# Fourier mixing followed by an ELU layer, one core: exponentials moved ahead of fold copies and conversions in ScalarE's order of the first sixteen steps

## Chip, cores and metric

The kernel runs on one core of one Trainium2 chip. The metric is the device time of one execution in microseconds (us). The kernel before took 1987.27 us in the median of three runs (1987.22 to 1990.91). The profiled execution, a run of its own, took 1994.49 us and its profile spans 1992.7 us.

## The reference

```python
X = np.fft.fft(x, axis=1)            # x: 8 x 3008 x 256
X = np.fft.fft(X, axis=2).real       # rows of 256, 24064 of them
h = X.reshape(B * S, D) @ w_in       # 256 -> 2048
g = np.where(h > 0.0, h, np.exp(np.minimum(h, 0.0)) - 1.0)
return (g @ w_out).astype(np.float32)    # 2048 -> 256
```

The two weight matrices arrive as 64-bit floats and are turned into 32-bit floats by the kernel itself.

## The kernel before, in words

**Stages.** For each batch of 3008 rows, the rows are folded by symmetry (additions and subtractions of loaded rows), and a Fourier transform along the sequence is made as matrix products with cosine and sine tables. Its results go into ring buffers in SBUF (Rr and Ir, with Rb for one channel more). The transform along the 256 channels is folded into the first weight matrix: products of channel tables with w_in give Wc and Ws ("fold chunk", L367), which ScalarE copies out of PSUM (put_chunk, L381) and of which one row is sent through DRAM to become the column vector wex (spread_last_row, L386: a transfer wx, then a transfer wex that waits for it).

**Steps.** The main loop has 376 steps. A step takes 256 columns of a ring and two of the sixteen blocks of 128 hidden units: matmuls P and Q (L693, L698) make the even and odd parts H in PSUM, VectorE makes E (L710) between them and the difference (h_minus, L720) after them, ScalarE makes two Relu (below_plus, below_minus) and two exponentials (exp_plus, exp_minus), and VectorE makes two ELU results (g_plus, g_minus, L736). Two steps after its start the results are multiplied by w_out into the PSUM accumulators pA to pD. Steps from 16 on use a scheme with seven products and four sums on GpSimd (L767 to L781); steps 0 to 15 are "side by side": two column tiles take turns, and each multiplies plainly (mm_plain, L803), pA and pB for one tile, pC and pD for the other. Tiles share buffers: PSUM bank M is single, H has three banks.

**Conversions.** In steps 0 to 14 the 64-bit weights are converted, one chunk of 256 hidden units in most steps (class Chunk, L173): `fields` (two VectorE operations, L211 and L217), `power` (three ScalarE operations), `round` (GpSimd, L359), `scale` (VectorE L254, then GpSimd L359). Chunk c of w_out is needed by the plain matmuls that stand in step 2c+2.

**Order.** Every call is an event with a due time in units of a step T = 4.8 (`at`, L1010); the events are sorted by due time (L1270) and the compute instructions of each engine run in that order. The due times are only a sorting key. Waits between engines are semaphores set by the program's dependences. DMA issues are not pinned, so that a scheduler places them: on SyncE's queue (SP) and, for the indirect loads of x and for the first chunk's wx and wex, on GpSimd's.

**Other work in the first 28 steps.** The odd transform of batch 0 (R_odd) goes through pA and pB ahead of their use by the main loop. Batch 1 is loaded (load_x, L137) and folded on GpSimd in 38 pieces spread over steps (begin_folds, L1192; loop from L1237 on). A separate path makes the transform of one channel for all batches (the "extra rows"): GpSimd adds two rows rx (L1212), SyncE spreads them and then gathers single channels of x with sixteen slow transfers (load_ext, L554), writes them to DRAM and reads them back as xs; GpSimd makes xe from xs (fold_ext, L587, due in step 25), and TensorE transforms xe (dft_ext, L612, at the end of step 25).

Of the kernel before, what the change touches and what calls it, by code (L numbers as in the profile page):

```python
# [77 lines left out]
def kernel(  # L78
# [58 lines left out]
    def load_x(b):  # L137
        L = [
            spool.tile([128, 6 * ND], FP, tag=f"xl{j}", bufs=1, name=f"xl{j}")
            for j in range(4)  # L140
        ]
        for j in (2, 1):
            c = 1 if j == 2 else 2 if b == NB - 1 else 0
            nc.gpsimd.indirect_dma_start(
                out=L[j],
                out_offset=None,
                in_=xflat,
                in_offset=bass.IndirectOffsetOnAxis(
                    ap=ix[:, c : c + 1].bitcast(U32), axis=0
                ),  # L150
                element_offset=b * SEQ * ND,
            )
        nc.sync.dma_start(out=L[3], in_=xrows(b, HALF, 6, 128))
        nc.sync.dma_start(out=L[0], in_=xrows(b, 0, 6, 128))
        if b == NB - 1:
            nc.gpsimd.dma_start(
                out=L[1][0:1, 0 : 5 * ND], in_=xrows(b, SEQ - 5, 1, 1, 5)
            )
        return L
# [184 lines left out]
    def bank(tag):  # L344
        bufs = 3 if tag == "H" else 1
        return ppool.tile([128, 512], FP, tag=tag, bufs=bufs, name=tag)
# [20 lines left out]
    def fold_chunk(c):  # L367

        q, half = divmod(c, 2)
        ps = folds[c] = bank("H")  # L370
        for n, part in enumerate((128, 0)):
            for h in range(2):
                mm(
                    ps[:, 256 * n : 256 * n + 256],
                    CC[:, h * 256 + part : h * 256 + part + 128],
                    w1[q][:, h, half * 256 : half * 256 + 256],
                    n == 0 and h == 0,
                    h == 1,
                )

    def put_chunk(c):  # L381
        cols = slice(c * 256, (c + 1) * 256)
        for n, dst in enumerate((Ws, Wc)):
            act(dst[:, cols], folds[c][:, 256 * n : 256 * n + 256])

    def spread_last_row(q):  # L386
        c = slice(q * 256, (q + 1) * 256)
        queue = nc.sync if q else nc.gpsimd
        queue.dma_start(out=wx_dr[:, c], in_=Ws[127:128, c])
        with nc.allow_non_contiguous_dma(reason="one row to columns"):  # L390
            queue.dma_start(
                out=wex[:, 2 * q : 2 * q + 2],
                in_=wx_dr[:, c].rearrange("o (f p) -> p (o f)", p=128),
            )
# [263 lines left out]
    def spread_ext(b, kodd):  # L658
        for sl, a, z in ring_cut(b * HALF + kodd * RUN, RUN, False):
            a, z = a + kodd * RUN, z + kodd * RUN  # L660
            nc.sync.dma_start(
                out=Rb[:, sl],
                in_=r128_dr[b : b + 1, a:z].to_broadcast([128, z - a]),
            )
            nc.sync.dma_start(out=Ir[127:128, sl], in_=r128_dr[b : b + 1, a:z])
# [137 lines left out]
    def mm_plain(i, a):  # L803

        S = steps[i]
        q = i // 8
        if i % 8 == 0 and a == 0:
            tiles[q] = Tile()
            tiles[q].acc = [bank(t) for t in ACC[2 * q : 2 * q + 2]]
        for n, (half, sign) in enumerate(((0, a), (1, 1 - a))):  # L810
            for r in range(2):
                mm(
                    tiles[q].acc[a][:, n * TW : (n + 1) * TW],
                    w2b(i, r, half),
                    blk(S, 2 * sign + r),
                    i % 8 == 0 and n == 0 and r == 0,
                    i % 8 == 7,
                )
        if a:
            del steps[i]  # L820
# [181 lines left out]
    def dft_now(d, par, tag):  # L1002
        d.mms(par, bank(tag))

    R_even, I_even = Dft(0, 0, 0, EO[0]), Dft(1, 0, 0, EO[2])
    R_odd, I_odd = Dft(0, 0, 1, EO[1]), Dft(1, 0, 1, EO[3])
# [3 lines left out]
    def at(t, fn):  # L1010
        events.append((t, len(events), fn))
# [58 lines left out]
    T = PERIOD  # L1070
    for chunk, k in (
        (w2_chunks[0], 0),
        (w1_chunks[2], 1),
        (w1_chunks[3], 2),
        (w2_chunks[1], 3),
        (w1_chunks[4], 4),
        (w2_chunks[2], 5),
        (w1_chunks[5], 6),
        (w2_chunks[3], 7),
        (w1_chunks[6], 8),  # L1080
        (w2_chunks[4], 9),
        (w1_chunks[7], 10),
        (w2_chunks[5], 11),
        (w2_chunks[6], 12),
        (w2_chunks[7], 14),
    ):
        t = k * T + 1.0
        at(t, chunk.fields)
        at(t + 0.02, chunk.power)
        at(t + 0.05, chunk.round)  # L1090
        at(k * T + (3.7 if k else 1.9), chunk.scale)
    for chunk, t in (
        (w1_chunks[6], 0.95),
        (w1_chunks[7], 2.2),
# [6 lines left out]
    for c in range(1, 8):  # L1101
        t = max(2 * c - 3, c % 3) * T + 4.7 if c > 1 else 2.3
        at(t, lambda c=c: fold_chunk(c))
        t = max(2 * c - 2, 3) * T + 1.4 if c > 1 else 3.0
        at(t, lambda c=c: put_chunk(c))
        at(t + 0.01, lambda c=c: spread_last_row(c))
    for i in range(8):
# [11 lines left out]
    for slot in range(total):  # L1119
        i = slot % 2 * 8 + slot // 2 if slot < 16 else slot  # L1120
        t = slot * T
        for dt, fn in (
            (0.0, mm_P),
            (0.9, even_part),
            (2.17, mm_Q),
            (3.55, h_minus),
            (4.2, below_plus),
            (4.8, below_minus),
            (T + 1.5, exp_plus),
            (T + 2.2, g_plus),  # L1130
            (T + 2.21, exp_minus),
            (T + 2.9, g_minus),
        ) + (
            (
                (2 * T + 0.87, lambda i: mm_plain(i, 0)),
                (2 * T + 3.04, lambda i: mm_plain(i, 1)),
            )
            if i < 16
            else WINOGRAD
        ):  # L1140
            at(t + dt, lambda fn=fn, i=i: fn(i))
# [12 lines left out]
    for q in range(2, n_tiles):  # L1154
        t = (8 * q + 9) * T
# [6 lines left out]
    def safe(col):  # L1162

        return 8 * ((col - 1 - RING) // TW) + 8 if col > RING else 0
# [16 lines left out]
    def at_dft(step, gap, b, ri, kodd, stat):  # L1181
        box = []

        def d():
            if not box:
                box.append(Dft(ri, b, kodd, stat()))
            return box[0]

        at_half(step, d, 1, 0)
        at_half(step + gap, d, 0, b * HALF + (kodd + 1) * RUN)  # L1190

    def begin_folds(b):  # L1192
        state["EO"], state["ops"] = fold_x(state["L"], lambda key: nc.gpsimd, 2)

    steps_b = HALF * 8 // TW
    for t, fn in (
        (-1.8, I_even.copy),
        (0.0, I_even.plus),
        (0.1, I_even.minus),
        (3.1, lambda: dft_now(R_odd, 1, "pA")),  # L1200
        (3.2, lambda: dft_now(R_odd, 0, "pB")),
        (T + 0.95, R_odd.copy),
        (T + 1.0, R_odd.plus),
        (T + 1.1, R_odd.minus),
    ):
        at(t, fn)
    at_half(4, lambda: I_odd, 1, 0)
# [6 lines left out]
    for n in range(16):  # L1214
        j, k = divmod(n, 4)
# [13 lines left out]
    n_big = sum(k[0] not in "czx" for k, _ in fold_keys)  # L1229
    for b in range(1, NB):  # L1230
        s0 = (b - 1) * steps_b
        l0 = s0 - 8 if b > 1 else 7.2
        at(l0 * T + 0.1, lambda b=b: state.update(L=load_x(b)))
        f0, f1 = (s0 - 1, s0 + 38) if b > 1 else (11, 37)
        at(f0 * T, lambda b=b: begin_folds(b))
        n = 0
        for key in fold_keys:  # L1237
            at(
                int(f0 + n * (f1 - f0) / n_big) * T + 1.3,
                lambda key=key: state["ops"][key](),  # L1240
            )
            n += key[0][0] not in "czx"
        for n, (ri, kodd) in enumerate(((0, 0), (1, 0), (0, 1), (1, 1))):
            at_dft(
                s0 + (28, 34, 38, 42)[n], 2, b, ri, kodd,
                lambda k=2 * ri + kodd: state["EO"][k],
            )
        for kodd in range(2):
            step = s0 + (28, 38)[kodd]
            assert step >= safe(b * HALF + (kodd + 1) * RUN)  # L1250
            at(step * T + 1.0, lambda b=b, kodd=kodd: spread_ext(b, kodd))
# [50 lines left out]
```

## Time and profile before

| quantity | us |
|---|---|
| span of the profiled execution | 1992.7 |
| TensorE matmuls busy | 1963.4 |
| VectorE busy | 1263.0 |
| ScalarE busy | 870.0 |
| GpSimd busy | 1330.9 |
| TensorE busy between 50 and 150 | 92.73 of 100 |
| TensorE busy between 150 and 186 | 36.00 of 36 |
| TensorE busy between 186 and 222 | 30.13 of 36 |
| TensorE busy between 400 and 800 | 400.00 of 400 |

A line of the timeline gives the start, the duration, the engine, the line of the kernel, the operation, the tile written and the tiles read, the count that was merged, and in square brackets how long the engine had been idle and what ended that. PE is TensorE, DVE VectorE, ACT ScalarE, POOL GpSimd, SPq the DMA issues of SyncE. A matmul of 32-bit floats shows as two records, and records overlap because the pipeline does: the pace is read from start to start. A line of the waits reads: who waited, for what, microseconds in total, times, the longest.

### The profile page before, as it was taken

The numbers are of one execution on the slowest core, as the hardware profiler recorded it, in microseconds if no ns is written. First come the engines' busy times: TensorE is split into PE (matmuls) and PEld (weight loads), VectorE is DVE, ScalarE is ACT, GpSimd is POOL, SyncE is SP. The second block draws the span as 40 slices with busy tenths as digits, with TensorE's granted clock in tenths as the row PEclk, the third lists the DMA queues.
The fourth block names the chain that finished last, engine by engine and source line by source line (L and its number), as shares of the span: only waits on it lengthen the run. The fifth ranks groups of instructions, "written<-read, shape, count | busy, mean of one in ns | idle before, by whom it ended". The sixth has DMA issues, their size and how long they took to land.

```text
span 1992.7 us, 26822 instructions
## 1 busy us (share of the span) xinstructions
PE 1963.4 (99%) x8896; PEld 1664.4 (84%) x8896; DVE 1263.0 (63%) x2322; ACT 870.0 (44%) x1666; POOL 1330.9 (67%) x1804
## 2 busy tenths in 40 slices
PE   8999999999999999999999999999999999999998
PEld 5777888888888888888888888888888888888887
DVE  6565656666566665666666765666556665566665
ACT  3553434444344434444434443444434444344443
POOL 3377757777487765777567775677757776455655
PEclk9999999999999999999999999999999999999999
DMA  9147401120101211011101211002010110100101
GB/s 352 33 20 13 106 11 17 27 75 16 16 15 37 59 23 18 16 46 44 26 14 19 59 29 28 12 19 83 11 21 12 19 22 14 16 12 12 22 10 23
DMA packets 255740, 71.08 MB, mean 36 GB/s; under 512 B 244255, under 2 KB 245044, under 8 KB 255090
## 3 DMA queue, kind: packets, MB, share of 16 engines
q1 hardware_dynamic: 251026, 56.53, 15.1%
q0 software_dynamic: 2400, 12.59, 1.9%
q8 instruction: 70, 1.15, 0.2%
q14 instruction: 68, 0.56, 0.1%
q10 hardware_dynamic: 2176, 0.26, 0.1%
HBM read 44.50 MB, written 24.80 MB: 35 GB/s over the span
## 4 chain that ended last, share of the span: by engine, by line
PE 90%; DMA 3%; DVE 2%; SPq 2%; ACT 1%; issue 1%; POOL 1%; POOLq 0%; DVEq 0%; ACTq 0%
PE H L350 36%; PE pB L350 15%; PE pD L350 15%; PE pC L350 15%; PE pA L350 8%; SPq L560 1%; DMA x<-in_x_dram 1%; DMA xl<-in_x_dram,ix 1%; DVE E L710 1%; SPq L920 0%; DMA wx<-Ws 0%; SPq L577 0%; DVE G L720 0%; POOL w L359 0%; ACT pow L362 0%
## 5 line engine op out<-in xcount | busy, mean ns | idle before, releaser
L359 POOL TENSOR_TENSOR G<-G 128x256 f32<-128x256 f32 x1440 | 1036.5, 729 | 565.4 <-DVE G L736 454.8
L710 DVE SCALAR_TENSOR_TENSOR E<-Rb,wex,H 128x256 f32<-128x256 f32 x752 | 327.8, 477 | 617.0 <-PE H L350 612.4
L362 ACT ACTIVATE G<-H 128x512 f32<-128x512 f32 x376 | 224.6, 597 | 946.1 <-DVE G L720 946.1
L350 PE MATMUL H<-Ir,Ws 128*128 128x256 f32 x1504 | 387.6, 380 | 3.7 <-DVE E L710 3.7
L350 PE MATMUL H<-Rr,Wc 128*128 128x256 f32 x1504 | 387.0, 380 | 0.0
L350 PE MATMUL pC<-G,WT 128*128 128x256 f32 x1440 | 369.5, 379 | 0.0
L350 PEld LDWEIGHTS H<-Rr,Wc 128*128 128x128 f32 x1504 | 285.6, 190 | 54.6 <-issue 3.1
L350 PEld LDWEIGHTS H<-Ir,Ws 128*128 128x128 f32 x1504 | 278.0, 189 | 53.2 <-DVE E L710 6.2
L350 PEld LDWEIGHTS pC<-G,WT 128*128 128x128 f32 x1440 | 273.6, 190 | 37.2
L736 DVE SCALAR_TENSOR_TENSOR G<-G,H 128x512 f32<-128x512 f32 x376 | 255.8, 680 | 53.8 <-ACT G L362 53.8
L720 DVE SCALAR_TENSOR_TENSOR G<-E,H 128x512 f32<-128x512 f32 x376 | 257.1, 684 | 37.7 <-POOL G L359 2.5
L736 DVE SCALAR_TENSOR_TENSOR G<-M,G 128x512 f32<-128x512 f32 x376 | 256.8, 683 | 0.0
L350 PE MATMUL pA<-G,w 128*128 128x256 f32 x784 | 230.9, 381 | 8.6 <-POOL w L359 6.5
L362 ACT ACTIVATE G<-G 128x512 f32<-128x512 f32 x376 | 233.3, 620 | 0.0
L350 PE MATMUL pD<-G,w 128*128 128x256 f32 x784 | 229.3, 379 | 0.0
L350 PE MATMUL pB<-G,w 128*128 128x256 f32 x784 | 229.3, 379 | 0.0
L362 ACT ACTIVATE M<-G 128x512 f32<-128x512 f32 x376 | 223.9, 596 | 0.0
L362 ACT ACTIVATE M<-M 128x512 f32<-128x512 f32 x376 | 220.9, 587 | 0.1
L350 PE MATMUL pB<-G,WT 128*128 128x256 f32 x720 | 214.5, 380 | 1.6 <-POOL G L359 1.6
L350 PE MATMUL pD<-G,WT 128*128 128x256 f32 x720 | 214.4, 379 | 1.5 <-DVE v L356 1.5
L350 PEld LDWEIGHTS pA<-G,w 128*128 128x128 f32 x784 | 149.0, 191 | 31.1 <-POOL w L359 10.9
L350 PEld LDWEIGHTS pD<-G,w 128*128 128x128 f32 x784 | 149.0, 190 | 20.3
(127 smaller groups left out, 1370.7 us busy)
## 6 DMA issues: line engine op xcount, KB each, us to landing
out_dram<-ot SPq DMA_DIRECT2D x496, 32.0 KB
xl<-in_x_dram SPq DMA_DIRECT2D x16, 768.0 KB
MC<-dft_mats SPq DMA_DIRECT2D x4, 1131.0 KB
out_dram<-ot SPq DMA_DIRECT2D x256, 2.0 KB
Rb<-r SPq DMA_DIRECT2D x10, 376.0 KB
raw<-in_moe_w_in_dram SPq DMA_DIRECT2D x7, 512.0 KB
raw<-in_moe_w_out_dram SPq DMA_DIRECT2D x5, 512.0 KB
out_dram<-ot SPq DMA_DIRECT2D x64, 28.0 KB
```

Source lines behind the costliest of these rows:

```text
L350: nc.tensor.matmul(out_, lhsT=lhsT, rhs=rhs, start=start, stop=stop, skip_group_check=True)
L359: pin(nc.gpsimd.tensor_tensor(out=o, in0=a, in1=b, op=op))
L362: pin(nc.scalar.activation(out=o, in_=i, func=func, **kw))
L560: nc.sync.dma_start(out=t[:, s0:s1], in_=bass.AP(tensor=xt, offset=x.offset + row * ND + 128, ap=[[SEQ * ND, NB], [step * ND, s1 - s0], [1 ...
L710: nc.vector.scalar_tensor_tensor(out=S.E[:, c], in0=Rb[:, cols(i)], scalar=wex[:, f : f + 1], in1=S.H[:, c], op0=ALU.mult, op1=ALU.add,)
L720: nc.vector.scalar_tensor_tensor(out=two(S.G[:, 0:512])[:, :, ::-1], in0=two(S.E), scalar=2.0, in1=two(S.H), op0=ALU.mult, op1=ALU.subtract,)
L736: nc.vector.scalar_tensor_tensor(out=o, in0=e, scalar=-1.0, in1=h, op0=ALU.add, op1=ALU.max)
```

## The change

Six edits, all in due times. (1) `fields`, `power`, `round` and `scale` of a conversion in step k move from 1.0, 1.02, 1.05 and 3.7 of that step to -0.5, 0.05, 0.06 and 2.95. (2) put_chunk and spread_last_row of chunks 2 to 7 move from 1.4 to 0.03 of their step. (3) For steps 0 to 15, exp_plus moves from T+1.5 to T+0.01 and exp_minus from T+2.21 to T+0.02. (4) The two halves of the odd transform move from 3.1 and 3.2 to T+0.5 and T+2.5, its copy from T+0.95 to T+2.6, its sum and difference from T+1.0 to T+4.2. (5) Batch 1's load moves from step 7.2 to 5.2. (6) Its folds are spread from step 8 on instead of step 11 on, to step 37 in both.

```diff
-        t = k * T + 1.0
-        at(t, chunk.fields)
-        at(t + 0.02, chunk.power)
-        at(t + 0.05, chunk.round)
-        at(k * T + (3.7 if k else 1.9), chunk.scale)
+        t = k * T
+        at(t - 0.5 if k else 0.95, chunk.fields)
+        at(t + 0.05 if k else 0.96, chunk.power)
+        at(t + 0.06 if k else 0.97, chunk.round)
+        at(t + 2.95 if k else 1.9, chunk.scale)
...
-        t = max(2 * c - 2, 3) * T + 1.4 if c > 1 else 3.0
+        t = max(2 * c - 2, 3) * T + 0.03 if c > 1 else 3.0
         at(t, lambda c=c: put_chunk(c))
         at(t + 0.01, lambda c=c: spread_last_row(c))
...
-            (T + 1.5, exp_plus),
+            (T + 0.01 if slot < 16 else T + 1.5, exp_plus),
             (T + 2.2, g_plus),
-            (T + 2.21, exp_minus),
+            (T + 0.02 if slot < 16 else T + 2.21, exp_minus),
...
-        (3.1, lambda: dft_now(R_odd, 1, "pA")),
-        (3.2, lambda: dft_now(R_odd, 0, "pB")),
-        (T + 0.95, R_odd.copy),
-        (T + 1.0, R_odd.plus),
-        (T + 1.1, R_odd.minus),
+        (T + 0.5, lambda: dft_now(R_odd, 1, "pA")),
+        (T + 2.5, lambda: dft_now(R_odd, 0, "pB")),
+        (T + 2.6, R_odd.copy),
+        (T + 4.2, R_odd.plus),
+        (T + 4.21, R_odd.minus),
...
-        l0 = s0 - 8 if b > 1 else 7.2
+        l0 = s0 - 8 if b > 1 else 5.2
...
-        f0, f1 = (s0 - 1, s0 + 38) if b > 1 else (11, 37)
+        f0, f1 = (s0 - 1, s0 + 38) if b > 1 else (8, 37)
```

In the order that results, each engine runs the same compute instructions as before. On ScalarE a side-by-side step now reads: two exponentials of the step before, fold copies, the conversion's three operations, then the two Relu of its own step. On VectorE the conversion's L254 comes ahead of h_minus instead of behind it, and `fields` ahead of E instead of behind it. On TensorE the odd transform's first half stands between P and Q of step 1 and its second half between Q of step 1 and P of step 2; both stood ahead of P of step 1. On SyncE the raw load of w_in's chunk 7 now comes ahead of the wex transfer of chunk 1, and batch 1's two row loads come behind it. On GpSimd one indirect load of batch 2 (L144) now stands between the xs and the xe operations of the extra rows, and the second one a step ahead of the two rx operations of step 28 instead of behind them.

## The prediction on record

> **What bounds the kernel now.** I read the page first, then TensorE's waits, then the timeline where those waits lie. On the page TensorE is busy for nearly all of the span:
>
> ```profile
> span 1992.7 us, 26822 instructions
> PE 1963.4 (99%) x8896; PEld 1664.4 (84%) x8896; DVE 1263.0 (63%) x2322; ACT 870.0 (44%) x1666; POOL 1330.9 (67%) x1804
> ```
>
> So 1992.7 - 1963.4 = 29.3 us of idle TensorE is all that an edit of order can win; the change alters no matmul. The waits name the larger pieces:
>
> ```profile
> PE pA L350 <- POOL w L359: 6.5, 5, 1.7
> PE H L350 <- POOL xe L359: 4.3, 1, 4.3
> PE H L350 <- DVE E L710: 3.7, 5, 1.4
> PE pA L350 <- DVE G L736: 2.1, 1, 2.1
> PE pB L350 <- POOL G L359: 1.6, 2, 1.1
> ```
>
> The first line is five waits of the plain matmuls for a converted chunk of w_out, at 60.07, 75.36, 90.29, 104.32 and 120.75 us (1.53, 1.04, 0.68, 1.67, 1.53). How one comes about is seen in step 9, in the timeline:
>
> ```profile
> 96.99 1.00 DVE L211 TENSOR_SCALAR pow<-raw 128x512 int32<-128x512 int32 x1
> ...
> 98.02 0.72 ACT L362 ACTIVATE pow<-pow,ebias 128x512 int32<-128x512 int32 x1 [1.21 <-DVE pow L211]
> ...
> 99.72 0.61 ACT L362 ACTIVATE G<-G 128x512 f32<-128x512 f32 x1
> ...
> 100.37 0.69 DVE L736 SCALAR_TENSOR_TENSOR G<-G,H 128x512 f32<-128x512 f32 x1 [2.05 <-ACT G L362]
> ...
> 102.17 0.68 DVE L254 SCALAR_TENSOR_TENSOR pow<-raw,pow 128x512 int32<-128x512 int32 x1
> ...
> 103.00 1.27 POOL L359 TENSOR_TENSOR w<-w,pow 128x512 f32<-128x512 f32 x1 [1.81 <-DVE pow L254]
> ...
> 104.32 0.48 PE L350 MATMUL pA<-G,w 128*128 128x256 f32 x1 [1.67 <-POOL w L359]
> ```
>
> ScalarE idles until `fields` is done, then runs the conversion, and only then the exponential; VectorE idles 2.05 for it, L254 follows two ELU and h_minus, GpSimd's product comes last, and TensorE waits. One other stretch matters before it, and one after. In step 2, E waits for wex, a transfer:
>
> ```profile
> 33.10 0.31 SPq L389 DMA_DIRECT2D wx<-Ws  x1
> 33.52 0.39 SPq L193 DMA_DIRECT2D raw<-in_moe_w_in_dram  x1
> 33.96 1.07 SPq L153 DMA_DIRECT2D xl<-in_x_dram  x1
> 40.28 0.37 SPq L391 DMA_DIRECT2D wex<-wx  x1
> 44.84 0.87 DVE L710 SCALAR_TENSOR_TENSOR E<-Rb,wex,H 128x256 f32<-128x256 f32 x2 [1.42 <-DMA wex<-wx]
> ```
>
> In step 25 TensorE waits for xe, the end of a chain that starts with rx (GpSimd until 127.59) and then takes 67 us of SyncE and transfers:
>
> ```profile
> 127.62 0.24 SPq L654 DMA_DIRECT2D r<-rx  x1
> 193.87 0.38 POOL L359 TENSOR_TENSOR xs<-xs 128x96 f32<-128x96 f32 x1 [6.31 <-DMA xs<-xe_dr]
> 194.67 4.18 PE L350 MATMUL H<-MC,xe 128*8 128x377 f32 x24 [4.25 <-POOL xe L359]
> ```
>
> **What the Trainium skill says.** "TensorE: Matmul & The Clock Gate", section "Part 1: The HAM clock gate", says that the array falls to half clock after an idle window of about 3.4 us, and that the windows of 3413 ns run freely. The trace agrees: the granted clock is 0.50 between 44 and 46 us and between 194 and 200 us, after the waits of 2.11 and 4.25; after 1.5 to 1.7 it stays 1.00. Four records that take 0.865 from start to start elsewhere took 1.63 at 198.78. "SBUF — State Buffer", section "SBUF: two separate sides", says that VectorE and GpSimd can lock each other out of a shared port for an instruction; L211 takes 0.42 here in most steps and 1.00 in step 9, so I allow some tenths per step for it.
>
> **Part 1, conversions and exponentials (edits 1 to 3).** They add nothing; 13 conversions and 16 pairs of exponentials change place on ScalarE and VectorE. In an odd step, from P to the next step's pA, TensorE issues P 0.87, plain 1.73, Q 0.87, plain 1.73, fold or transform 1.73 to 1.9, P 0.87: 7.8 us. `fields` is now done before P ends. ScalarE does the two exponentials within about 0.7 after P's start, then the three conversion operations (1.8), so GpSimd's `round` ends at about 3.8. VectorE does E (after P, until 1.9), two ELU (1.2) and L254 (0.7), until 3.8; the product takes 1.3, until 5.1. That is 2.7 before pA asks, so all five waits should go: 6.45. After each, pA took 1.83 to the next start where 1.73 is normal: 5 x 0.1. Three small ones have the same cause in VectorE's and ScalarE's lateness: 0.28 ahead of the fold at 116.39, 0.13 at 136.53, 0.70 + 0.1 at 139.22. Sum **-8.15**. The other side: L254 now stands ahead of h_minus, so h_minus to h_minus is a loop through ScalarE: 0.71 to the first Relu, then 0.49, 0.52, 0.52 to the end of the exponentials' issue, fold copies 0.53, Relu of pow 0.65, L254 0.62, with gaps some 4.6 us. The shortest step is 5.2, so it is hidden, with 0.6 in hand. Put_chunk moves with its two transfers; wex is then needed two steps later (over 10 us; there wex can be issued 1.1 us after wx, 55.33 and 56.46), so nothing.
>
> **Part 2, start (edit 4).** Moving the odd transform lets P, Q and the first plain matmuls come earlier: P of step 1 at 32.5, pA's plain part from 38.9 to 40.6. It gains nothing, because Q of step 2 needs E, and E needs wex. The raw load now ahead of wex waits for conversion 1 (`round` at about 38.4), before wx lands at 40.26, so it does not delay the issue. Behind wx stand then two raw loads (1.0 MB) instead of one raw and one xl (1.3 MB); at the 400 GB/s that this stretch shows that is 0.7 earlier, Q at 45.0. But TensorE now idles in one piece, 40.6 to 45.0, instead of 0.96, 2.11 and 0.37. At half clock it then loses half of 3 to 5 us, 1.5 to 2.5, where before it lost about 0.4 after Q. I take +1.7 - 0.7 = **+1.0**, ends -0.5 and +2.5.
>
> **Part 3, the xe chain.** The chain's start moves with rx. GpSimd's `round` of conversion 12 ends at about 116.4, one fold half 1.0 and rx 2.36 follow: 119.7, so 7.9 earlier (part 2 shifts both alike). TensorE arrives 8.15 earlier: +0.3. The indirect load moved between xs and xe costs its 1.02 and its 0.27 of idle on the path: +1.3. Sum **+1.6**: the wait of 4.25 grows to about 5.9. This is what is given back; the cold clock after it is there before too, and its length (a window more or less, +-1.7) goes into the range.
>
> **Part 4, folds (edits 5, 6).** 38 pieces over 29 steps instead of 26; GpSimd is busy 6.5 of 20 us in 80 to 100, so the early ones are hidden. After the chain, the second indirect load is ahead of rx, and rx (1.92) is a step later. The wait at 219.47 (1.12, 1.38 with the refill) should go and some 0.5 come back a step later: **-0.9**. The one at 211.43 comes from ScalarE behind the DVE rx and stays.
>
> **Sum.** -8.15 + 1.0 + 1.6 - 0.9 = -6.45 on 1992.7, 1986.2 for a profiled span. The three timed runs are some 7 us below the profiled one. I take the same difference from their median: 1987.27 - 6.45 = 1980.8. Should the timed runs not have the xe wait at all (4.25 and about 3 of half clock would make up those 7 us), part 3 drops out, and the gain is 8.
>
> **Rivals.** (a) *The xe wait swallows the gain.* If rx doesn't move forward with TensorE, because GpSimd, which is 97% busy from 120 on, is held by the added folds, each microsecond won ahead of step 25 is waited there. For it: the chain takes 67 us whatever TensorE does. Against: six fold halves stand ahead of rx instead of three, but four of them come by step 10, where GpSimd is mostly idle, and two instead of three in the busy stretch. With rx only 3 to 5 earlier the time is 1984 to 1988, say 1985.5. (b) *Slower: the serial loop sets the step.* If L254 ahead of h_minus makes the loop ScalarE-VectorE longer than a step, TensorE waits for P, Q or plain operands in each of 13 conversion steps. Its price is 13 times the excess over 5.2 to 7.1. It decides from an excess of 0.5 on (6.5 us, the whole gain), and at 0.9, a loop of about 7 us, the time is 1987.3 - 6.45 + 11.7 = 1992.5. Against: the loop adds up to 4.6, and locks of VectorE show at most 0.7 for one L254. (c) *More is won:* the clock windows fall well in step 2 and 25, or the xe wait isn't in timed runs: 1977. (d) *The order doesn't follow the due times:* excluded for pinned compute, whose new order I read from the built program.
>
> **How the numbers follow.** Forecast 0.60, around 1980.8 (1978 to 1983.3). (c) 0.10. (a) 0.21, 1983.3 to 1991. (b) 0.09, above 1991. A measurement of this kernel can tell about 0.2%, 4 us, from no change: faster is below 1983.3: 0.60 + 0.10 = 0.70; same 0.21; slower 0.09. The range leaves out (b) and the far ends of (a) and (c): 1975.5 to 1988.
>
> **What would show it.** Right: no wait of pA for POOL w between 55 and 125; an exponential right behind the Relu on ScalarE; one wait of 4 to 5 us ending near 45 at Q, with the clock at 0.5 after it; rx ended near 120; the xe wait 5 to 6 with an indirect load of x between xs and xe. Wrong: waits of H for E or of h_minus for L254 in each step (b), or an xe wait of 8 and more (a).

## The result, and the profile after

The kernel after took 1977.83 us in the median of four runs (1977.65 to 1980.5), the kernel before beside it 1987.5 (1987.22 to 1990.91): a ratio of 0.9951, with a 95% interval of 0.9933 to 0.9968. The gain of 9.7 us is about 3 us more than predicted. The time lies just below the forecast's own 1978 to 1983.3, close to the 1977 of rival (c), and inside the outer range of 1975.5 to 1988. Of the profiled executions the span went from 1992.7 to 1978.7, 14.0 less; where the other 4.3 come from is shown below.

The waits of TensorE in the kernel after (who waited, for what, total, times, longest, in us):

```profile
PE H L350 <- DVE E L710: 6.7, 3, 4.4
...
PE pB L350 <- POOL G L359: 0.5, 1, 0.5
PE pA L350 <- POOL w L359: 0.2, 1, 0.2
```

Of the five waits for a converted chunk (6.5) 0.2 are left. The line for xe (4.3) is gone, the one for E has grown from 3.7 to 6.7, and GpSimd's G from two waits (1.6) to one (0.5).

Step 9 in the timeline after, the stretch that the prediction showed of before:

```profile
96.11 0.71 ACT L362 ACTIVATE pow<-pow,ebias 128x512 int32<-128x512 int32 x1
...
97.77 0.68 DVE L254 SCALAR_TENSOR_TENSOR pow<-raw,pow 128x512 int32<-128x512 int32 x1
97.98 1.62 POOL L359 TENSOR_TENSOR w<-raw,w 128x512 f32<-128x512 f32 x1 [0.98 <-ACT w L362]
98.37 0.68 DVE L720 SCALAR_TENSOR_TENSOR G<-E,H 128x512 f32<-128x512 f32 x1
...
99.58 0.60 ACT L362 ACTIVATE M<-G 128x512 f32<-128x512 f32 x1
...
99.90 1.17 POOL L423 TENSOR_TENSOR e<-xl 128x381 f32<-128x381 f32 x1
100.09 0.62 ACT L362 ACTIVATE G<-G 128x512 f32<-128x512 f32 x1
...
101.04 1.26 POOL L359 TENSOR_TENSOR w<-w,pow 128x512 f32<-128x512 f32 x1
...
102.35 0.92 PE L350 MATMUL pA<-G,w 128*128 128x256 f32 x3 [0.20 <-POOL w L359]
```

ScalarE's conversion starts without idle time, L254 stands ahead of h_minus (L720), and the first exponential (100.09) follows right behind the two Relu (the second at 99.58). The product is done at 102.30 although two fold operations that edit 6 put here (until 101.07) stand ahead of it: that is the 0.2. Without them, right behind `round` (99.60), it would by an estimate have ended at about 100.9, 1.2 before pA asked at 102.15. The products ahead of pA's starts at 61.66, 75.64 and 89.62 ended 1.9, 2.5 and 1.7 before, and the one ahead of 116.73, behind two fold operations and four sums of GpSimd, 0.4 before.

The groups of VectorE and ScalarE between 50 and 125 us, after (busy time and mean ns, then the idle time before):

```profile
L710 DVE SCALAR_TENSOR_TENSOR E<-Rb,wex,H 128x256 f32<-128x256 f32 x22 | 9.6, 477 | 19.7 <-PE H L350 19.7
L254 DVE SCALAR_TENSOR_TENSOR pow<-raw,pow 128x512 int32<-128x512 int32 x7 | 8.2, 1165 | 0.0
...
L736 DVE SCALAR_TENSOR_TENSOR G<-G,H 128x512 f32<-128x512 f32 x11 | 7.5, 679 | 0.0
...
L362 ACT ACTIVATE pow<-pow,ebias 128x512 int32<-128x512 int32 x10 | 7.2, 717 | 0.0
...
L362 ACT ACTIVATE G<-H 128x512 f32<-128x512 f32 x10 | 6.0, 598 | 24.6 <-DVE G L720 24.6
```

Two of the same groups before:

```profile
L736 DVE SCALAR_TENSOR_TENSOR G<-G,H 128x512 f32<-128x512 f32 x10 | 6.9, 687 | 24.0 <-ACT G L362 24.0
...
L362 ACT ACTIVATE pow<-pow,ebias 128x512 int32<-128x512 int32 x10 | 7.2, 722 | 17.3 <-DVE pow L211 17.3
```

Before, VectorE idled 24.0 us ahead of L736 for ScalarE's exponential, ScalarE 17.3 ahead of the conversion's first operation for `fields`, and VectorE only 6.8 ahead of E for TensorE. Now VectorE's idle time is for TensorE (19.7 ahead of E), and ScalarE's is for h_minus, ahead of the first Relu (24.6; before 14.5). L254 went from 683 to 1165 ns; the last section comes back to it.

The start of step 2 after, in the timeline:

```profile
33.25 0.31 SPq L389 DMA_DIRECT2D wx<-Ws  x1
...
33.67 5.90 SPq L193 DMA_DIRECT2D raw<-in_moe_w_in_dram  x2
...
40.09 0.37 SPq L391 DMA_DIRECT2D wex<-wx  x1
...
45.49 0.87 DVE L710 SCALAR_TENSOR_TENSOR E<-Rb,wex,H 128x256 f32<-128x256 f32 x2 [4.18 <-DMA wex<-wx]
...
46.41 2.07 PE L350 MATMUL H<-Ir,Ws 128*128 128x256 f32 x4 [4.39 <-DVE E L710]
```

A stretch from 45.80 on in the view by stretches of the same kernel (length, then the busy time of PE, PEld, DVE, ACT and POOL, the granted clock, the DMA share and GB/s):

```profile
45.80:52.62 6.82, 6.21 (x15) 4.95 (x16) 4.88 (x9) 2.12 (x4) 1.27 (x1) 0.50 0.45 164
```

E waits for wex, Q for E, and 6.82 us at half clock follow. And the extra rows in the timeline, whose last link made TensorE wait 4.25 before:

```profile
123.11 0.24 SPq L654 DMA_DIRECT2D r<-rx  x1
...
175.90 0.36 SPq L583 DMA_DIRECT2D xs<-xe_dr  x1
...
182.05 0.39 POOL L359 TENSOR_TENSOR xs<-xs 128x96 f32<-128x96 f32 x1
...
182.59 1.03 POOL L144 DMA_INDIRECT xl<-in_x_dram,ix  x1
...
183.63 0.53 POOL L359 TENSOR_TENSOR xe<-xs 128x48 f32<-128x48 f32 x2
...
185.03 2.09 PE L350 MATMUL H<-MC,xe 128*8 128x377 f32 x24
```

From the first transfer to the issue of the last read-back it took 52.8 us; before, 63.9 (127.62 to 191.52). So xe was ready before TensorE came.

Starts of the same matmuls on TensorE, in the two profiled executions:

| start of | before | after | difference | in this stage |
|---|---|---|---|---|
| P of step 3 | 50.55 | 53.88 | +3.33 | +3.33: wex and half clock |
| the last pD ahead of xe's matmuls | 189.82 | 184.50 | -5.32 | -8.65: conversion steps |
| the first pA after xe's matmuls | 200.41 | 188.01 | -12.40 | -7.08: xe wait 4.25 and half clock |
| pB at 219.47 before | 219.47 | 205.79 | -13.68 | -1.28: folds |

The rest of the program adds 0.3 to the gain. The third row takes pA, as in the kernel before the half clock lasts through P, until 200.14.

### The profile page after: what moved, and what is told of

Read it like the earlier page. It is cut to its first block, busy times and chain, and to the rows that moved or that the text cites. A ratio compares the mean times of both kernels' runs of the same rounds, so it can differ in the third digit from the quotient of the medians.

```text
span 1978.7 us, 26821 instructions
## 1 busy us (share of the span) xinstructions
PE 1960.0 (99%) x8896; PEld 1665.0 (84%) x8896; DVE 1273.9 (64%) x2322; ACT 869.4 (44%) x1666; POOL 1333.9 (67%) x1804
## 4 chain that ended last, share of the span: by engine, by line
PE 96%; DVE 1%; DMA 1%; POOL 1%; issue 0%; ACT 0%; POOLq 0%; DVEq 0%; ACTq 0%
PE H L350 39%; PE pD L350 16%; PE pB L350 16%; PE pC L350 16%; PE pA L350 8%; DMA xl<-in_x_dram,ix 1%; DMA wx<-Ws 0%; DVE E L710 0%; DMA wex<-wx 0%; POOL G L359 0%; DVE v L356 0%; DVE e L423 0%; DVE o L423 0%; DVE Ir L356 0%; DVE G L736 0%
## 5 line engine op out<-in xcount | busy, mean ns | idle before, releaser
L720 DVE SCALAR_TENSOR_TENSOR G<-E,H 128x512 f32<-128x512 f32 x376 | 257.3, 684 | 37.5 <-PE H L350 1.9
L736 DVE SCALAR_TENSOR_TENSOR G<-G,H 128x512 f32<-128x512 f32 x376 | 256.0, 681 | 24.9 <-ACT G L362 24.8
L736 DVE SCALAR_TENSOR_TENSOR G<-M,G 128x512 f32<-128x512 f32 x376 | 257.2, 684 | 0.0
L350 PEld LDWEIGHTS pB<-G,w 128*128 128x128 f32 x784 | 150.1, 192 | 20.8
```

The source lines that it names most:

```text
L350: nc.tensor.matmul(out_, lhsT=lhsT, rhs=rhs, start=start, stop=stop, skip_group_check=True)
L720: nc.vector.scalar_tensor_tensor(out=two(S.G[:, 0:512])[:, :, ::-1], in0=two(S.E), scalar=2.0, in1=two(S.H), op0=ALU.mult, op1=ALU.subtract,)
L736: nc.vector.scalar_tensor_tensor(out=o, in0=e, scalar=-1.0, in1=h, op0=ALU.add, op1=ALU.max)
```

## The experiments

All are compared with the kernel before, run beside them.

**Edits 1 to 3 alone** (conversions, put_chunk, exponentials; the first three hunks of the change, as printed above).

> The kernel before with edits 1 to 3 alone (conversions, fold copies and exponentials earlier). Theory (the waits of pA for the converted w_out chunks are the gain): those five waits are gone, TensorE reaches step 25 some 8 us earlier, and the time falls by 7 to 9 us, to about 1979.5. Rival (the xe chain swallows what is won ahead of it unless the folds move too): the xe wait grows by what was won, and the time falls by 3 us or less, to 1984.5 or more.

1980.45 us in the median of 5 against 1988.19, ratio 0.9963 (0.9950 to 0.9977): -7.7. Two lines of its waits:

```profile
PE pB L350 <- POOL G L359: 1.6, 2, 1.1
...
PE pA L350 <- POOL w L359: 0.8, 1, 0.8
```

The waits for w fall from 6.5 to 0.8, those for GpSimd's G stay. No wait for xe. The gain is that of part 1. The 0.8 is ahead of a pA in step 11; GpSimd's product stands there behind four sums and three fold operations, one of which edit 6 takes out of this place.

**Edit 4 alone** (the odd transform).

```diff
-        (3.1, lambda: dft_now(R_odd, 1, "pA")),
-        (3.2, lambda: dft_now(R_odd, 0, "pB")),
+        (T + 0.5, lambda: dft_now(R_odd, 1, "pA")),
+        (T + 2.5, lambda: dft_now(R_odd, 0, "pB")),
...
```

> The kernel before with edit 4 alone (odd transform split around step 1). Theory (E of step 2 waits for wex whatever stands ahead of it): Q of step 2 starts within 1 us of 45.8, the idle time before it becomes one piece and the half clock after it longer, and the time is the same or up to 2 us longer: 1987.5 to 1989.5. Rival (the wait of 2.11 us for g_minus is a loss of its own): 2 us shorter, 1985.5.

1988.88 in the median of 13 against 1988.19, ratio 1.0003 (0.9994 to 1.0011): no difference that can be told. From its timeline:

```profile
45.90 2.08 PE L350 MATMUL H<-Ir,Ws 128*128 128x256 f32 x4 [4.90 <-DVE E L710]
```

The idle time is in one piece, as predicted. The five waits for w (6.1) stay.

**Edits 5 and 6 alone** (batch 1's load and folds).

```diff
-        l0 = s0 - 8 if b > 1 else 7.2
+        l0 = s0 - 8 if b > 1 else 5.2
...
-        f0, f1 = (s0 - 1, s0 + 38) if b > 1 else (11, 37)
+        f0, f1 = (s0 - 1, s0 + 38) if b > 1 else (8, 37)
```

> The kernel before with edits 5 and 6 alone (batch 1 loaded and folded earlier). Theory (only GpSimd's order around steps 25 to 28 counts): the five waits for w stay, the wait at 219 us of the kernel before is gone, and the time falls by 1 to 2 us, to about 1986. Rival (earlier folds free GpSimd and pull the xe chain forward): the xe chain starts 3 us earlier and the time falls by 4 us or more, to 1983.5 or less.

1987.89 in the median of 13, ratio 1.0001 (0.9992 to 1.0010). The lowest run is 1986.09, that of before 1987.21. In the profile the wait at 219.47 is gone and the five for w stand (6.5). The profile shows the wait removed; the time doesn't resolve the 1 to 2 us, since 4 of the 13 runs lie over 4 us above the lowest.

**The change without edit 4** (the lines of the second experiment put back).

> The changed kernel with the odd transform where it was before (edits 1, 2, 3, 5, 6). Theory (edit 4 only gathers the idle time ahead of Q of step 2 into one piece and so costs half clock): 1 to 2 us shorter than the changed kernel, about 1976.3, with a single half-clock window of 3.4 us or none in 40 to 55 us. Rival (edit 4 is part of the gain): about 1979.8, 2 us longer than the changed kernel.

1978.38 in the median of 5, ratio 0.9955 (0.9941 to 0.9969), as the whole change. In its profile Q of step 2 waits 2.95 instead of 4.39, yet half clock lasts the same 6.8 us. Neither expectation came: the time is 2 us above the one and 1.4 below the other, and there were two half-clock windows. So the split neither wins nor costs anything that these runs can tell. Against the first experiment it has the folds' edits in addition and its median is 2.1 lower, which five runs of each don't resolve.

**Edit 3 alone** (exponentials) and **edits 1 and 2 alone** (conversions and put_chunk).

```diff
-            (T + 1.5, exp_plus),
+            (T + 0.01 if slot < 16 else T + 1.5, exp_plus),
...
-            (T + 2.21, exp_minus),
+            (T + 0.02 if slot < 16 else T + 2.21, exp_minus),
```

> The kernel before with edit 3 alone (exponentials of steps 0 to 15 ahead of fold copies and conversions). Theory (the chain conversion, exponential, two ELU, h_minus, L254, product is cut by either edit, so the two overlap): waits of pA for w fall from 6.5 to under 2 us and the time falls by 5 to 7 us, to about 1982. Rival (the edits add up): about half of edits 1 to 3, 4 us, 1984.

> The kernel before with edits 1 and 2 alone (conversions and fold copies earlier, exponentials where they were). Theory (either edit cuts the chain): waits of pA for w under 2 us, the time falls by 5 to 7 us, to about 1982. Rival (the edits add up): 4 us, 1984.

The exponentials alone: 1980.44 in the median of 9 against 1987.56, 0.9963 (0.9952 to 0.9973), -7.1, with 1.3 of waits for w left. The conversions alone: 1981.68 in the median of 20, 0.9973 (0.9964 to 0.9983), -5.9, with 0.6 left. The two add to 13.0 while both together gave 7.7: they cut the same chain (`fields`, conversion, exponential, ELU, L254, product, pA) at two places, and either cut is nearly enough; in all three profiles only the wait in step 11 is left. Of the conversions' runs 7 of 20 lie over 4 us above the lowest.

**xe taken one step later, in the kernel before.** Its matmuls and what follows them move from step 25 to 26.

```diff
-    at(25 * T + 4.75, dft_ext)
+    at(26 * T + 4.75, dft_ext)
...
```

> The kernel before with the transform of xe, and what follows it, one step later (step 26 instead of 25, 4.75 us of matmuls). Theory (the xe wait of the profile of before is not in most executions): the median within 1 us of 1988, with fewer runs above 1990. Rival (the xe wait is in every execution and the gain of the change is partly its removal): 4 us or more shorter, 1984 or less.

1986.28 in the median of 14 against 1987.56, ratio 0.9992 (0.9984 to 1.0000): 1.3 less. Its profile caught a long chain again (66.2 us), and the wait didn't go; it moved:

```profile
196.10 0.39 POOL L359 TENSOR_TENSOR xs<-xs 128x96 f32<-128x96 f32 x1 [8.61 <-DMA xs<-xe_dr]
196.57 0.53 POOL L359 TENSOR_TENSOR xe<-xs 128x48 f32<-128x48 f32 x2
197.06 3.01 POOL L359 TENSOR_TENSOR G<-G 128x256 f32<-128x256 f32 x4
...
199.32 1.22 PE L350 MATMUL pB<-G,WT 128*128 128x256 f32 x2 [7.25 <-POOL G L359]
```

GpSimd's fold_ext was still due in step 25 and waits in order, so the main loop's sums G stand behind it, and pB behind them. This edit therefore moves the wait and can't remove it, and the rival's gain of 4 us could not have come by it. What tells is the spread: the profiled execution took 1996.25, the other 13 runs 1985.93 to 1988.79. The median is 1.7 below the 1988 expected; where the 1.3 come from was not settled.

**wx and wex of chunk 1 on ScalarE's queue, in the kernel after.**

```diff
-        queue = nc.sync if q else nc.gpsimd
+        queue = nc.scalar if q == 1 else nc.sync if q else nc.gpsimd
```

> The changed kernel with both transfers of wex's chunk 1 issued from ScalarE's queue, which is empty, instead of SyncE's, where four large loads stand ahead. Theory (the wait of 4.4 us ahead of Q of step 2 and the half clock after it are due to wex alone): wx lands in 2 to 3 us, E of step 2 starts at 41 us or before, no half clock in 40 to 55, and the time is 5 to 7 us below the changed kernel, about 1972. Rival (the 16 transfer engines are full until 46 us and no queue lands earlier; and ScalarE, waiting for wx, is late with its Relu): the same time, 1977.8, or up to 2 us more.

1979.35 in the median of 11, ratio 0.9963 (0.9952 to 0.9974): no better than the kernel after. From its timeline (ACTq is ScalarE's issue of transfers):

```profile
33.04 0.49 ACTq L389 DMA_DIRECT2D wx<-Ws  x1
...
37.38 0.39 ACTq L391 DMA_DIRECT2D wex<-wx  x1
37.82 0.60 ACT L362 ACTIVATE G<-H 128x512 f32<-128x512 f32 x1 [4.54 <-DMA wx<-Ws]
...
42.12 1.97 PE L350 MATMUL pA<-G,w 128*128 128x256 f32 x8 [2.04 <-ACT bs L362]
...
45.84 0.87 DVE L710 SCALAR_TENSOR_TENSOR E<-Rb,wex,H 128x256 f32<-128x256 f32 x2 [1.03 <-DMA wex<-wx]
...
46.76 1.13 PE L350 MATMUL H<-Ir,Ws 128*128 128x256 f32 x4 [2.68 <-DVE E L710]
```

wex is issued 2.7 earlier than on SyncE and E starts no earlier: the rival's account. The Trainium skill, "DMA: Bandwidth & Descriptors", section "Issuing engines are not separate DMA queues", says that transfers of the scalar, sync and gpsimd queues run on the same 16 engines and interleave; this run agrees. ScalarE stood idle for 4.54 us while it held the issue, and a pA of TensorE waited 2.04 for ScalarE.

**Batch 1's first loads held back, in the kernel after**, and then **the raw loads of w_in's chunks 6 and 7 as well.** GpSimd clears one element of each buffer first, so that the load waits for GpSimd's place in the order. What is computed stays the same.

```diff
+        if b == 1:
+            for j in range(4):
+                pin(nc.gpsimd.memset(L[j][0:1, 0:1], 0.0))
...
+            if self in (w1_chunks[6], w1_chunks[7]):
+                pin(nc.gpsimd.memset(home[0:1, 0:1], 0.0))
...
-        (w1_chunks[6], 0.95),
-        (w1_chunks[7], 2.2),
+        (w1_chunks[6], 3.1),
+        (w1_chunks[7], 3.11),
```

> The changed kernel with batch 1's four loads (3.1 MB) held back by a small GpSimd write to each of their buffers, so that they start at about 65 us. Theory (wex of chunk 1 waits for bytes ahead of it and beside it on the 16 transfer engines): the wait ahead of Q of step 2 falls from 4.4 to about 2 us, and the time to about 1975. Rival (the latency of two dependent small transfers sets it, whatever else is in flight): wex lands at 44 us or later as before, same time, 1977.8.

> As e9_xl_late, and the raw loads of w_in's chunks 6 and 7 held back likewise to step 3. Theory: wex is issued as soon as wx has landed and nothing large is ahead of it; it lands by 40 us, the wait ahead of Q of step 2 is under 1 us, no half clock in 40 to 55, and the time is 5 to 7 us below the changed kernel, about 1971.5. Rival (latency): at most 2 us below, 1976 or more.

The first: 1975.45 in the median of 4 against 1988.35, ratio 0.9934 (0.9918 to 0.9949); Q of step 2 waits 1.99. wex took 3.3 us from its issue to landing, where it was 5.3 in the kernel after. Its issue (39.56) was late for another reason than wx: it stood on SyncE's queue behind a raw load that waited for L254 until 39.04. The second edit takes away that load too. With both: 1972.86 in the median of 5 (1972.69 to 1975.56), ratio 0.9917 (0.9904 to 0.9931), against 0.9944 (0.9931 to 0.9958) of the kernel after in the same comparison. From the timeline of the second (line numbers are 5 higher):

```profile
33.11 0.31 SPq L394 DMA_DIRECT2D wx<-Ws  x1
...
35.36 0.86 DVE L715 SCALAR_TENSOR_TENSOR E<-Rb,wex,H 128x256 f32<-128x256 f32 x2
...
35.76 0.37 SPq L396 DMA_DIRECT2D wex<-wx  x1
...
36.28 1.13 PE L355 MATMUL H<-Ir,Ws 128*128 128x256 f32 x4 [0.85 <-DVE E L715]
...
41.10 0.86 DVE L715 SCALAR_TENSOR_TENSOR E<-Rb,wex,H 128x256 f32<-128x256 f32 x2
```

wex can be issued 2.65 us after wx instead of 6.84, E of step 2 starts at 41.10 with no wait, where it was 45.49, and no half clock follows. This version beats both kernels: its slowest run lies below the fastest of the kernel after. Its profiled run, at 1975.35 one of its two slower ones, has the xe wait again:

```profile
179.79 2.31 PE L355 MATMUL H<-MC,xe 128*8 128x377 f32 x24 [2.15 <-POOL xe L364]
```

TensorE arrives there 7.3 us earlier than in the kernel after, and the chain of the extra rows took 59.6 us.

**The same with rx a step earlier.**

```diff
-    at(12 * T + 1.35, lambda: ext_rows(1, gtt, 1))
-    at(12 * T + 2.0, lambda: spread_ext(0, 1))
+    at(11 * T + 3.0, lambda: ext_rows(1, gtt, 1))
+    at(11 * T + 3.1, lambda: spread_ext(0, 1))
```

> As e10_loads_late, and the two rx operations, which start the xe chain, due at 11T+3.0 instead of 12T+1.35. Theory (the xe chain has its own, changing length, and only its long executions make TensorE wait): rx ends 4 us or more earlier, the median is that of e10_loads_late within 1 us, and fewer runs lie 4 us and more above the lowest. Rival (the chain holds TensorE in most executions once more is won ahead of it): the median is 3 us or more below e10_loads_late.

A miss: 1984.41 in the median of 13, ratio 0.9981 (0.9973 to 0.9989), 11.5 above the version without it. From its timeline:

```profile
113.28 0.24 SPq L394 DMA_DIRECT2D wx<-Ws  x1
...
113.61 7.91 SPq L565 DMA_DIRECT2D x<-in_x_dram  x4
...
121.62 2.61 SPq L396 DMA_DIRECT2D wex<-wx  x1
...
129.56 2.07 PE L355 MATMUL H<-Ir,Ws 128*128 128x256 f32 x4 [8.24 <-DVE E L715]
```

The gathers of x got between wx and wex of chunk 7 on SyncE's queue, and Q of step 14 waits 8.24 us. Half clock lasts from within this wait to 132.89, a loss of about 1.7 (half of the 3.3 us of work in it), so that the two make up 9.9 of the 11.5. The chain of the extra rows was earlier (its last read-back was issued at 162.80), but this run can't say what that alone is worth; an earlier rx with wex ahead of it wasn't tried.

**The kernel after once more,** beside the last three.

> The changed kernel again, beside the three above. Theory: median 1977 to 1979; runs 2 to 4 us above the lowest differ in the half-clock windows near 46 us, and a run 6 us above by the xe wait. Rival (the gain was that of one stretch of runs): 1981 or more.

1979.6 in the median of 5 (1976.39 to 1982.0), the ratio given above: a little over the 1977 to 1979 expected and below the rival's 1981. In its profile Q of step 2 waits 5.05, half clock lasts 3.4 us, and there is no xe wait.

## Why the prediction came out as it did

**Part 1 (-8.15): right in mechanism and size.** The profiled steps gained 8.65, edits 1 to 3 alone 7.7. That either of two cuts would have been nearly enough, the prediction didn't say. The exponentials follow the Relu, the waits for w go from 6.5 to 0.2. Rival (b), the serial loop through ScalarE and VectorE, fell: in the stretch of 50 to 125 us neither E nor h_minus made TensorE wait by more than 0.2 (ahead of Q at 96.70), and VectorE has 19.7 us of idle time for TensorE ahead of E. The products end 1.7 to 2.5 ahead of three of the five pA where 2.7 was argued and 0.4 ahead of the one in step 11, and in step 9 the added folds take all of it. The margin of the loop was smaller too: "locks of VectorE show at most 0.7 for one L254" held for the old order, and in the new one an L254 took up to 1.65, 0.97 over its usual 0.68.

**Part 2 (+1.0): right in mechanism, the size off in the profiled execution.** The idle time is in one piece and ends with wex. Predicted was Q at 45.0 and 1.5 to 2.5 lost at half clock. Q came at 46.41, as wex took 5.4 us from issue to E instead of the 3.8 that the predicted 0.7 gain needs, and half clock lasted 6.8 us. Q was 0.64 later than before instead of 0.7 earlier, and from Q to P of step 3 it took 2.69 longer, where 1.7 was predicted: +3.33 in all, outside the upper end of 2.5. How much half clock follows differs from one execution of the kernel after to the next (6.8 and 3.4 us in its two profiles; the last section shows on what it depends). Over many runs the cost is less: edit 4 alone measured +0.7 with an interval that covers zero, and taking it out of the change altered nothing that the runs can tell.

**Part 3 (+1.6): the step that failed.** "The wait of 4.25 grows to about 5.9" didn't happen; the wait was 0. The start of the chain was right: rx's first transfer came 4.5 earlier in spite of the 3.33 lost at the start, 7.8 by the steps alone, where 7.9 was predicted. What failed is "67 us of SyncE and transfers" as a fixed length. From rx's first transfer to the issue of the last read-back it took 63.9 in the profile before, 66.2 in that of the experiment with xe a step later, and between 49.0 and 59.6 in the other twelve, with the same transfers. So the wait is in some executions and not in others. That it was missing in most of the timed ones is argued from times, as these left no trace: the profiled execution before took 7.2 more than the median, about what the wait and its half clock cost it (7.08); of 45 runs of the kernel before beside experiments 5 to 8, 5 lie over 4 us above the lowest; with xe a step later one of 14 does, the one whose profile has the long chain. What makes the chain long was not settled. The indirect load between xs and xe took 1.03 as predicted, but lay ahead of TensorE's arrival and cost nothing. With the loads held back, where TensorE waits 2.15 for xe, it is on the path as predicted (1.01, with 0.29 of idle time ahead of it). Rival (a) needed rx not to move forward; it moved, and the rival fell. That version shows, though, that the wait can return when more is won ahead of it.

**Part 4 (-0.9): right, a little more.** The wait at 219.47 went and the 0.5 that was to come back a step later didn't: -1.28 in the profile. The medians don't resolve it: 2.1 between the change without edit 4 and edits 1 to 3 alone, 0.3 between the folds' edits alone and the kernel before.

**The sum.** -6.45 had +1.6 of part 3 in it. The alternative in the prediction, that part 3 drops out if the timed runs don't have the xe wait, is also one case of its rival (c), and it fits what came: it gives 8, and a part 4 of 1.28 instead of 0.9 gives 8.4; 9.7 was measured in the first comparison, and 8.8 between the medians of the second (1988.35 and 1979.6). For the profiled pair the same sum was off by 7.5 (-6.45 against -14.0): part 3 by 8.7 (-7.08 in place of +1.6), and against it part 2 by 2.3. The weak link was to carry a difference worked out on one execution over to the median of others; the timed runs came nearer to the sum because most of them, as argued above, lacked the xe wait before and after, and not because part 3 was right: to that extent it was luck.

## What to carry to other kernels

On an engine that works in order, put what the next engine waits for ahead of work that is due later, and expect two cuts of one chain to win once, not twice. Before a wait of a profiled execution is priced, compare that execution's time with the others: 7 us more said that this wait was not in all of them. A small dependent transfer behind large loads was helped here by holding back the loads, not by another queue, and whatever moves ahead on its queue has to be looked at too.

## What was not expected of the hardware

- **Half clock comes in pieces, and the length of a wait doesn't tell how many.** Apart from the end of an execution, all stretches at 0.50 lasted one, two or three times 3.41 us. The same wait ahead of Q of step 2 with edits 1 to 3 alone, and in the change without edit 4:

```profile
46.27 1.13 PE L350 MATMUL H<-Ir,Ws 128*128 128x256 f32 x4 [2.87 <-DVE E L710]
```

```profile
45.48 2.07 PE L350 MATMUL H<-Ir,Ws 128*128 128x256 f32 x4 [2.95 <-DVE E L710]
```

No half clock followed the first and 6.8 us the second; elsewhere 4.39 gave 6.8 us, 5.05 gave 3.4, and 7.25 gave 10.2. What does tell is where a wait falls. In each of the 14 profiles the clock changes only at multiples of 3.41 us from its first change. Cut into windows there, from 26 us to the last matmuls, the traces show no exception: half clock began after a window in which TensorE was idle for 2.03 us or more (11 times), and never after one with 1.95 or less; it went on after a window with 0.62 or more and ended after one with 0.37 or less. The 2.87 lies in two windows (1.44 and 1.60 of idle time with the shorter waits near it), while 2.03 of the 2.95 lies in one. The Trainium skill, "TensorE: Matmul & The Clock Gate", section "Part 1: The HAM clock gate", says that the windows run freely, which agrees. It names an idle window of about 3.4 us as what lowers the clock; here 2.03 in a window was enough, so the wait of 2.11 in the kernel before, which the prediction took as agreeing, does not fit that figure.
- **A VectorE operation started behind GpSimd's waits for it.** In the timeline after:

```profile
77.41 1.30 POOL L359 TENSOR_TENSOR w<-raw,w 128x512 f32<-128x512 f32 x1 [4.31 <-ACT w L362]
77.83 1.43 DVE L254 SCALAR_TENSOR_TENSOR pow<-raw,pow 128x512 int32<-128x512 int32 x1
```

L254 ends 0.55 after GpSimd's `round` (78.71), near its own 0.68; alone it starts and ends within 0.68. The new order lets the two start together in most conversions, hence the mean of 1165 ns. The Trainium skill, "SBUF — State Buffer", section "SBUF: two separate sides", describes such a lock for operations with two inputs in SBUF; the trace agrees.
- **A chain of the same small transfers took 49 to 66 us** in executions of nearly the same program; the cause is open.
